# DMA transposes of the activations that read SBUF where they read a copy in HBM, with the last two blocks of channels overlapping

## The chip, the cores and the metric

The kernel runs on one core of a Trainium2 chip. The metric is device time in microseconds (us) from the first to the last instruction. Three runs of the kernel before gave 364.56, 364.61 and 364.64 us, a median of 364.61. The profiled execution, from which all durations below come, spans 364.9 us.

Engines: PE is TensorE (PEld its weight loads, which overlap with its matmuls), DVE is VectorE, ACT is ScalarE, POOL is GpSimd, SP is SyncE, which issues nearly all the DMAs of this kernel, one after the other in program order. SPq stands for SP's queue of instructions: the time that a DMA-issuing instruction holds SP.

## The reference

One sequence of 2048 tokens of 576 channels in bf16 goes through an attention block and an MLP block, each with a residual.

```python
def _A_ref(x, wqkv, wo):                 # x: layernormed input
    H = 32; Dh = D // H                  # D = 576, Dh = 18
    W, dil = 8, 2
    qkv = (x @ wqkv).reshape(B, S, 3, H, Dh).transpose(2, 0, 3, 1, 4)
    q, k, v = qkv[0], qkv[1], qkv[2]
    idx = pos[:, None] - off[None, :]    # off = 0, 2, ..., 14
    ...
    attn = softmax(where(mask, einsum("bhsd,bhswd->bhsw", q, kg) * Dh**-0.5, -1e9))
    return einsum("bhsw,bhswd->bhsd", attn, vg)... @ wo

def _B_ref(x, w1, b1, w2, b2):           # F = 4608
    h = gelu(layernorm(x) @ w1 + b1)
    return h @ w2 + b2

h  = x + _A_ref(layernorm(x), wqkv, wo)
h2 = h + _B_ref(layernorm(h), w1, b1, w2, b2)
```

## The kernel before

The 2048 tokens are 16 tiles of 128 tokens; token 16p + j is row p of tile j. A tile is handled with its tokens on the 128 partitions for layernorm, attention and the residual. Every matmul that contracts over the 576 channels (QKV, the output projection Wo, the first MLP product) needs the tile transposed: channels on the partitions, tokens in the free dimension. 576 is four blocks of 128 and one of 64. The kernel keeps a transposed tile as five blocks (`KT` = 5): four whole ones, and a fifth that holds channels 512 to 575 twice, once in each half of the partitions.

The matmuls work on halves of the PE array: each of them contracts 64 rows, and two of them, on the two halves of the rows (`half_rows(0)` and `half_rows(1)`), run beside each other into two different PSUM banks. `phase` (L210) issues them: in the first phase half r of the rows works for output half r, over five blocks; in the second the halves are swapped, over four blocks. The fifth block is needed in the first phase alone, and there each half of the partitions serves its own output half, which is why it holds the same 64 channels twice. The weights of these 64 channels lie in tiles of their own (`wqh_sb`, `woh_sb`, `w1h_sb`).

A transposed tile comes in one of two ways.

- On PE, for the eight even tiles of layernorm 1, the first two tiles of the attention output and the first two of layernorm 2: `transpose_in` (L178) makes five transposes of 128 columns into PSUM (L182), and where the source isn't yet doubled (`tail` is None) a sixth of 64 columns (L186). ACT or DVE copies the result to SBUF.
- By DMA, for the eight odd tiles of layernorm 1 (`xnT`), 14 tiles of the attention output (`oT`) and 14 of layernorm 2 (`hnT`). The tile is first stored to HBM with 640 columns: the 576 channels (L193, or L284 for two tiles of `xnT` at once) and then channels 512 to 575 again (L194, L285). A DMA transpose reads the 640 columns back into the five blocks (L199, L430, L493; L288 for two tiles). It waits for both stores.

Order of the work: `manual_schedule` leaves every engine's program order as written. The QKV stage (0 to 71 us) loops over pairs of (tile, q/k/v) products, numbered `qd` 0 to 23; tables list what is issued `after` each of them. `out_x(i)` and `in_x(i)` are the stores and the transpose of the i-th pair of odd tiles; the products of pair i begin at `qd` 12 + 3i. Loads of the MLP's weights are interleaved, each paced by an ACT instruction. From 71 us on, eight groups of two tiles pass through MLP1 (`pm`), Wo of the next group (`pw`) and MLP2 (`po`), with the attention of the group after that on DVE, its output tiles c and d sent by `send_o` and `read_o` and their layernorm 2 by `ln2_send` and `ln2_ins`. `oT` has three buffers, `hnT` one, `xnT` five of two tiles each.

Two orders in the code matter for the steps below. In groups 3 to 6 SP's program has `send_o(c)`, a load of the attention's window (`halo`), `read_o(c)`, `send_o(d)`, `read_o(d)`. In `ln2_in` (L492) the first transpose of a pair waits, by a dependency put in by hand, for the last store of the pair.

Of the kernel before, what the change touches and what calls it, by code (L numbers as in the profile page):

```python
# [17 lines left out]
def kernel(  # L18
# [71 lines left out]
    wq_sb = qp.tile([P, KF, 3 * D], BF16, name="wq_sb")  # L90
    wqh_sb = qp.tile([P, 3, HALF], BF16, name="wqh_sb")
# [24 lines left out]
    def load_wqkv_half(engine, t, r):  # L116
        c0 = t * D + r * HALF
        engine.dma_start(out=wqh_sb[half_rows(r), t, :], in_=A_wqkv[KF * P:D, c0:c0 + HALF])

    def load_wo(qs):  # L120
        src = A_wo.rearrange("(h d) c -> h d c", h=H)
        for q in qs:
            load(wo_sb[q * H:(q + 1) * H, :, :], src[:, q:4 * KF:4, :])
            load(woh_sb[q * H:(q + 1) * H, :], src[:, 4 * KF + q % 2, q // 2 * HALF:(q // 2 + 1) * HALF])

    def load_w1h():
        load(b1_bf[:], B_b1.rearrange("(ft p) -> ft p", p=P))
        src = B_w1[KF * P:D, :].rearrange("p (u g c) -> p u g c", u=NU, g=2)
        for r in range(2):
            load(w1h_sb[half_rows(r), :].rearrange("p (u c) -> p u c", u=NU), src[:, :, r, :])  # L130

    def load_w1(c):
        cols = slice(c * F // 6, (c + 1) * F // 6)
        load(w1_sb[:, :, cols], B_w1[0:KF * P, cols].rearrange("(k p) c -> p k c", p=P))
# [7 lines left out]
    def ln_stats(srcs, tag, c1, c0, bufs, first=None, eps=True):  # L142
        n = len(srcs)
        pool = qp if tag.startswith("ln1") else sb
        stats = pool.tile([P, n, 2, nc.vector.BN_STATS_DIM], F32, tag=f"{tag}_stats", name=f"{tag}_stats", bufs=bufs)
# [32 lines left out]
    def transpose_in(pt, src, tail=None):  # L178
        for kt in range(KT):
            c = min(kt * P, D - P)  # L180
            if kt < KF or tail is None:
                nc.tensor.transpose(pt[:, kt, :], src[:, c:c + P], ident[:])  # L182
        if tail is not None:
            nc.tensor.transpose(pt[:, KF, :], tail[:].rearrange("p r c -> p (r c)"), ident[:])
            return
        nc.tensor.transpose(pt[0:HP, KF, :], src[:, KF * P:D], ident[:])  # L186


    stored = [None]

    def dma_out(src):
        td = dram.tile([P, KT * P], BF16, tag="td", name="td", bufs=4)
        nc.sync.dma_start(out=td[:, 0:D], in_=src)  # L193
        stored[0] = nc.sync.dma_start(out=td[:, D:KT * P], in_=src[:, KF * P:D]).ins  # L194
        return td

    def dma_transpose(dst, src):
        td = dma_out(src)
        nc.sync.dma_start_transpose(out=dst, in_=td[:])  # L199
# [9 lines left out]

    def phase(duo, swap, after):  # L210
        first = last = None
        n = len(duo["g"][0])
        for i in range(n):
            for kt in range(KF if swap else KT):
                for r in range(2):
                    lhsT, rhs = duo["op"](r ^ swap, i, half_rows(r), kt)
# [36 lines left out]
    xnT, xn_tail = {}, {}  # L253
# [7 lines left out]
    def tr_x(js, tag):  # L261
        pair = psum_pair(tag or "CAB"[(ring_pos[0] + 1) % 3], "xt_pt", BF16)
        for n, j in enumerate(js):
            transpose_in(tr_view(pair, n), q_all[:, j, :], xn_tail.pop(j, None))
# [12 lines left out]
    xd = [dram.tile([2, P, KT * P], BF16, name=f"xd{i}") for i in range(NT // 4)]  # L277

    def odd_x(i):
        return q_all[:, 4 * i + 1:4 * i + 4:2, :]  # L280

    def out_x(i):
        dst = xd[i][:, :, :].rearrange("j p c -> p j c")
        nc.sync.dma_start(out=dst[:, :, 0:D], in_=odd_x(i))  # L284
        nc.sync.dma_start(out=dst[:, :, D:KT * P], in_=odd_x(i)[:, :, KF * P:D])  # L285

    def in_x(i):
        nc.sync.dma_start_transpose(out=new_xnT(ODD[2 * i:2 * i + 2])[:],  # L288
                                    in_=xd[i][:, :, :].rearrange("j p c -> (j p) c"))
# [10 lines left out]
    def qkv_duo(j, t):  # L300
        def make():
# [3 lines left out]
            def op(g, i, sl, kt):  # L305
                c0 = t * D + g * HALF
                return xt[sl, kt, :], (wq_sb[sl, kt, c0:c0 + HALF] if kt < KF else wqh_sb[sl, t, :])
# [118 lines left out]
    def send_o(j):  # L426
        o_sent[j] = dma_out(q_all[:, j, :])

    def read_o(j):
        nc.sync.dma_start_transpose(out=new_oT(j)[:], in_=o_sent.pop(j)[:])  # L430

    pw_of, o_sent = {}, {}

    def wo_duo(j, tag):
        def make():
# [3 lines left out]
            def op(g, i, sl, kt):  # L439
                c0 = g * HALF  # L440
                return t[sl, kt, :], (wo_sb[sl, kt, c0:c0 + HALF] if kt < KF else woh_sb[sl, :])
# [39 lines left out]
    def ln2_send(j):  # L481
# [3 lines left out]
        hn[j] = dma_out(y[:])  # L485

    def ln2_out(j):
        hn[j] = dma_out(hn[j][:])
# [3 lines left out]
    def ln2_in(j):  # L492
        read[0] = nc.sync.dma_start_transpose(out=hnT_slot(j), in_=hn.pop(j)[:]).ins  # L493
        if stored[0] is not None:
            tc.add_manual_dep(read[0], stored[0].name, sync_dep, reason="stores ahead of the transposes of LN2")
            stored[0] = None
# [45 lines left out]
    def mlp1_duo(grp, us, tag):  # L542
        def make():
# [5 lines left out]
            def op(g, i, sl, kt):  # L549
                f0 = fts[g][i] * P  # L550
                c0 = (GF * us[i // GF] + i % GF) * P
                return (w1_sb[sl, kt, f0:f0 + P] if kt < KF else w1h_sb[sl, c0:c0 + P]), ht[sl, kt, 0:N]
# [198 lines left out]
    with tc.manual_schedule(engines={ENG.PE, ENG.Activation, ENG.DVE, ENG.SP, ENG.Pool}):  # L751
        load_x(EVEN[0:1])
        load_x(EVEN[1:2])
        for r in range(2):
            load_wqkv_half(nc.scalar, 1, r)
# [6 lines left out]
        for r in range(2):  # L762
            load_wqkv_half(nc.sync, 2, r)
# [4 lines left out]
        for r in range(2):  # L768
            load_wqkv_half(nc.sync, 0, r)
# [25 lines left out]
        def center(j, mean, op):  # L795
            nc.vector.tensor_scalar(out=q_all[:, j, 0:D if j in EVEN[:5] else KF * P],
# [296 lines left out]
```

## Time and profile before

| engine | busy us | share of the span |
|---|---|---|
| PE | 357.1 | 98% |
| PEld | 291.4 | 80% |
| DVE | 302.3 | 83% |
| ACT | 229.2 | 63% |
| POOL | 37.1 | 10% |
| profiled execution, span | 364.9 | |
| median of three runs | 364.61 | |

| stretch, us | PE busy us | DVE busy us | DMA share | GB/s |
|---|---|---|---|---|
| 0 to 10 (start) | 8.21 | 5.46 | 0.79 | 234 |
| 10 to 38 (QKV, even tiles) | 27.47 of 28 | 25.66 | 0.93 | 263 |
| 38 to 71 (QKV, odd tiles) | 31.31 of 33 | 30.19 | 0.92 | 245 |
| 71 to 256 (groups 0 to 4) | 185.00 of 185 | 172.04 | 0.37 to 0.56 | 77 to 163 |
| 256 to 328 (groups 5 and 6) | 71.58 of 72 | 59.66 | 0.28 to 0.42 | 61 to 81 |
| 328 to the end | 33.57 of 37 | 9.32 | 0.05 | 15 |

The granted TensorE clock is 1.00 in every stretch. The first table is the busy time of each engine, a sum over its instructions; the second the same by stage. PE is nearly always busy: what can be won without removing PE work is what it idles, 364.9 - 357.1 = 7.8 us in all, and most of that lies at the start and the end.

### The profile page before, as it was taken

The page shows a single profiled execution, that of the slowest core. Times are in us where ns is not written, and L with a number is a line of the kernel's source. Part 1 is how long each engine was busy: PE and PEld are TensorE (multiplying, and loading weights), DVE is VectorE, ACT ScalarE, POOL GpSimd, SP SyncE. Part 2 cuts the span into 40 slices and gives each one's busy share as a digit, 9 for nine tenths or more (in the row PEclk, how much of TensorE's full clock was granted, in tenths as well). Part 3 has the DMA queues.
Part 4 walks back from the last instruction along what each step waited for, and adds up shares of the span by engine and source line. Part 5 has one row for each costly group of instructions (what it writes and reads, how often), then busy time and mean ns, then how long its engine had stood idle before and what let it go on. Part 6 is the DMA issues. An engine that isn't in the chain of part 4 may idle for free.

```text
span 364.9 us, 11410 instructions
## 1 busy us (share of the span) xinstructions
PE 357.1 (98%) x4891; PEld 291.4 (80%) x4891; DVE 302.3 (83%) x422; ACT 229.2 (63%) x507; POOL 37.1 (10%) x47
## 2 busy tenths in 40 slices
PE   8999799999999999999999999999999999999996
PEld 5678687788778878887888778877887788778874
DVE  5899989999899998999899989998799999710431
ACT  4779655799555684468646954695469366805630
POOL 2141003000111020101010211020101100100000
PEclk9999999999999999999999999999999999999999
DMA  7979998984436743531353155503642342120001
GB/s 226 300 153 330 239 238 184 359 286 73 136 103 88 178 178 77 82 110 51 85 121 88 37 131 91 87 35 92 131 64 59 74 84 72 37 56 19 2 2 33
DMA packets 61907, 43.70 MB, mean 120 GB/s; under 512 B 31888, under 2 KB 60176, under 8 KB 61856
## 3 DMA queue, kind: packets, MB, share of 16 engines
q1 hardware_dynamic: 59968, 41.13, 42.2%
q0 software_dynamic: 1728, 1.77, 4.6%
q8 instruction: 38, 0.62, 0.7%
q10 hardware_dynamic: 160, 0.07, 0.1%
q14 instruction: 13, 0.11, 0.1%
HBM read 21.10 MB, written 12.42 MB: 92 GB/s over the span
## 4 chain that ended last, share of the span: by engine, by line
PE 92%; DMA 5%; SPq 1%; ACT 1%; issue 0%; DVE 0%
PE pm L217 38%; PE po L664 26%; PE pq L217 12%; PE po L576 10%; PE pw L217 5%; DMA oT<-td 2%; DMA wq_sb<-in_A_wqkv_dram 1%; DMA xnT<-xd 1%; DMA xd<-q_all 1%; SPq L104 1%; PE xt_pt L182 1%; ACT kv_ring L312 0%; PE h_pt L182 0%; PE o_pt L182 0%; ACT q_all L175 0%
## 5 line engine op out<-in xcount | busy, mean ns | idle before, releaser
L557 ACT ACTIVATE h_all<-pm,b_sb 128x256 f16<-128x256 f32 (+1 forms) x288 | 108.5, 497 | 69.7 <-PE pm L217 69.7
L217 PE MATMUL pm<-hnT,w_sb 64*128 64x256 bf16 x2304 | 143.0, 269 | 0.0
L217 PEld LDWEIGHTS <-w_sb 64*128 64x128 bf16 x2304 | 111.8, 94 | 15.0 <-issue 1.7
L664 PEld LDWEIGHTS <-h_all 128*128 128x128 f16 x512 | 49.4, 98 | 14.0 <-issue 1.6
L217 PE MATMUL pq<-wq_sb,xnT 64*128 64x288 bf16 x768 | 54.7, 283 | 3.1 <-DMA xnT<-xd 2.2
L217 PEld LDWEIGHTS <-xnT 64*128 64x128 bf16 x864 | 43.1, 94 | 13.0 <-DMA xnT<-xd 2.5
L348 DVE TENSOR_TENSOR prod<-prod 128x2304 bf16<-128x2304 bf16 (+1 forms) x64 | 44.2, 691 | 2.0
L394 DVE TENSOR_TENSOR prod<-kv_ring,probs 128x4608 bf16<-128x4608 bf16 x16 | 40.9, 2555 | 2.4 <-DMA kv_ring<-kv_dram 2.0
L342 DVE TENSOR_TENSOR prod<-kv_ring,q_all 128x4608 bf16<-128x4608 bf16 x16 | 40.8, 2549 | 0.5 <-DMA kv_ring<-kv_dram 0.3
L217 PE MATMUL pm<-hnT,w1h_sb 64*128 64x256 bf16 x288 | 39.2, 269 | 0.0
L664 PE MATMUL po<-w2a_sb,h_all 128*128 128x288 bf16 (+1 forms) x282 | 38.9, 286 | 0.0
L400 DVE TENSOR_TENSOR prod<-prod 128x2304 bf16<-128x2304 bf16 (+1 forms) x32 | 33.9, 1058 | 1.1
L576 PEld LDWEIGHTS <-h_all 128*128 128x128 bf16 x288 | 27.9, 98 | 7.9 <-issue 1.0
L664 PEld LDWEIGHTS <-kv_ring 128*128 128x128 f16 x252 | 24.6, 98 | 6.3
L478 POOL TENSOR_TENSOR ln_rstd<-ln_var,mhalf 128x1 f32<-128x1 f32 x13 | 12.0, 924 | 171.1 <-ACT ln_var L477 171.1
L576 PE MATMUL po<-w2a_sb,h_all 128*128 128x288 bf16 x224 | 28.5, 286 | 0.0
L664 PE MATMUL po<-w2b_sb,h_all 128*128 128x288 bf16 (+1 forms) x142 | 21.3, 286 | 0.0
L217 PE MATMUL pw<-wo_sb,oT 64*128 64x288 bf16 x256 | 19.6, 283 | 0.4 <-DMA oT<-td 0.4
L735 ACT COPY po<-po 128x288 f32<-128x288 f32 x18 | 6.9, 384 | 19.7 <-PE po L664 18.6
L644 DVE TENSOR_TENSOR kv_ring<-h_all 128x1536 f16<-128x1536 f16 (+3 forms) x9 | 6.8, 752 | 14.7 <-ACT h_all L557 14.7
L162 POOL TENSOR_TENSOR ln_rstd<-ln_veps,mhalf 128x1 f32<-128x1 f32 (+2 forms) x14 | 13.4, 967 | 50.3 <-DVE ln_veps L156 34.7
L217 PEld LDWEIGHTS <-oT 64*128 64x128 bf16 x288 | 13.6, 94 | 5.0 <-DMA oT<-td 1.2
(110 smaller groups left out, 387.3 us busy)
## 6 DMA issues: line engine op xcount, KB each, us to landing
w_sb<-in_B_w_dram SPq DMA_DIRECT2D x6, 768.0 KB, 5.9
kv_ring<-kv_dram SPq DMA_DIRECT2D x28, 144.0 KB, 2.8
w2a_sb<-in_B_w_dram SPq DMA_DIRECT2D x4, 1008.0 KB, 6.2
kv_dram<-kv_ring SPq DMA_DIRECT2D x13, 288.0 KB, 3.3
out_dram<-o_sb SPq DMA_DIRECT2D x15, 144.0 KB, 2.6
td<-q_all SPq DMA_DIRECT2D x14, 144.0 KB, 1.8
td<-hn SPq DMA_DIRECT2D x14, 144.0 KB, 1.8
x_all<-in_A_x_dram SPq DMA_DIRECT2D x12, 144.0 KB, 2.9
```

Source lines behind the costliest of these rows:

```text
L162: nc.gpsimd.tensor_tensor(out=rstd[:], in0=veps[:], in1=mhalf[:].to_broadcast([P, n]), op=ALU.pow)
L217: last = nc.tensor.matmul(duo["g"][r ^ swap][i], lhsT=lhsT, rhs=rhs, start=(swap == 0 and i == 0 and kt == 0), stop=(swap == 1 and kt == K ...
L342: nc.vector.tensor_tensor(out=prod[:], in0=k_ring[j % 2], in1=q_all[:, j, :].unsqueeze(1) .to_broadcast([P, W, D]), op=ALU.mult)
L348: nc.vector.tensor_tensor(out=prod[:, :, o * H:o * H + n], in0=prod[:, :, a * H:a * H + n], in1=prod[:, :, c * H:c * H + n], op=ALU.add)
L394: nc.vector.tensor_tensor(out=prod[:].rearrange("p w (d h) -> p w d h", h=H), in0=v_ring[j % 2].rearrange("p w (d h) -> p w d h", h=H), in ...
L400: nc.vector.tensor_tensor(out=prod[:, 0:n, :], in0=prod[:, 0:n, :], in1=prod[:, n:2 * n, :], op=ALU.add)
L478: nc.gpsimd.tensor_tensor(out=rstd[:], in0=var[:], in1=mhalf[:], op=ALU.pow)
L557: pace[0] = nc.scalar.activation(out=hT(grp)[:, f, 0:N], in_=ps[:, r, i * N:(i + 1) * N], func=ACT.Gelu_apprx_tanh, bias=b1_sb[:, f:f + 1] ...
L576: nc.tensor.matmul(banks[half], lhsT=hT(grp)[:, f, i * P:(i + 1) * P], rhs=w2_rows(f)[:, half * HALF:(half + 1) * HALF], start=(f == 0), s ...
L644: nc.vector.tensor_tensor(out=s_slot(t, m0, m1), in0=a, in1=b, op=alu)
L664: nc.tensor.matmul(bank, lhsT=l, rhs=r, start=start, stop=stop, skip_group_check=True)
L735: nc.scalar.copy(out=bank[seed[step][1]], in_=bank[seed[step][0]])
```

## The change

The DMA transposes read their tile in SBUF, without stores to HBM. Since the source has 576 columns and a transposed block has 128, each tile takes two instructions: columns 0 to 511 into blocks 0 to 3, and columns 448 to 575 into block 4. Channels 448 to 511 now are the ones held twice, in the upper half of block 3 and in the lower half of block 4. `transpose_in` makes five whole transposes for every tile on PE, and the sixth, of 64 columns, is gone.

`block(r, kt)` says which block half r of the rows reads at step kt, so that every product still has nine matmuls per half. The weights follow: `wq_sb` has a fifth block with rows 448 to 575 (one load of 128 partitions for two of 64 partitions and half the columns); `wo_sb` and `w1_sb` hold channels 512 to 575 in the upper half of their block 3, and `woh_sb` and `w1h_sb` hold channels 448 to 511. The load of `w1` is cut in four pieces of 864 KB with three blocks each and two pieces of 576 KB on 64 partitions, for six of 768 KB; the load of `wo` has two more DMAs.

On SP, a transpose is issued where the store was, or where the transpose was, as the diff shows. In SP's program the transposes of pair 0 of the odd tiles stand ahead of four stores of k and v to HBM, where the stores `out_x(0)` were. The dependency by hand in `ln2_in` is gone. The DVE writes each centred even tile in one instruction, where three of them had a second one for the doubled tail, and the statistics of layernorm 1 share buffers.

```diff
-    wq_sb = qp.tile([P, KF, 3 * D], BF16, name="wq_sb")
-    wqh_sb = qp.tile([P, 3, HALF], BF16, name="wqh_sb")
+    wq_sb = qp.tile([P, KT, 3 * D], BF16, name="wq_sb")
...
-    def load_wqkv_half(engine, t, r):
-        c0 = t * D + r * HALF
-        engine.dma_start(out=wqh_sb[half_rows(r), t, :], in_=A_wqkv[KF * P:D, c0:c0 + HALF])
+    def load_wqkv_last(engine, t):
+        engine.dma_start(out=wq_sb[:, KF, t * D:(t + 1) * D], in_=A_wqkv[D - P:D, t * D:(t + 1) * D])
...
     def load_w1(c):
-        cols = slice(c * F // 6, (c + 1) * F // 6)
-        load(w1_sb[:, :, cols], B_w1[0:KF * P, cols].rearrange("(k p) c -> p k c", p=P))
+        if c < 4:
+            cols = slice(c * F // 4, (c + 1) * F // 4)
+            load(w1_sb[:, 0:KF - 1, cols], B_w1[0:(KF - 1) * P, cols].rearrange("(k p) c -> p k c", p=P))
+        else:
+            r = c - 4
+            load(w1_sb[half_rows(r), KF - 1, :], B_w1[(KF - 1) * P + r * P:(KF - 1) * P + r * P + HP, :])
...
-    def transpose_in(pt, src, tail=None):
+    def transpose_in(pt, src):
         for kt in range(KT):
             c = min(kt * P, D - P)
-            if kt < KF or tail is None:
-                nc.tensor.transpose(pt[:, kt, :], src[:, c:c + P], ident[:])
-        if tail is not None:
-            nc.tensor.transpose(pt[:, KF, :], tail[:].rearrange("p r c -> p (r c)"), ident[:])
-            return
-        nc.tensor.transpose(pt[0:HP, KF, :], src[:, KF * P:D], ident[:])
+            nc.tensor.transpose(pt[:, kt, :], src[:, c:c + P], ident[:])
...
-    def dma_out(src):
-        td = dram.tile([P, KT * P], BF16, tag="td", name="td", bufs=4)
-        nc.sync.dma_start(out=td[:, 0:D], in_=src)
-        stored[0] = nc.sync.dma_start(out=td[:, D:KT * P], in_=src[:, KF * P:D]).ins
-        return td
-
     def dma_transpose(dst, src):
-        td = dma_out(src)
-        nc.sync.dma_start_transpose(out=dst, in_=td[:])
+        nc.sync.dma_start_transpose(out=dst[:, 0:KF, :], in_=src[:, 0:KF * P])
+        return nc.sync.dma_start_transpose(out=dst[:, KF:KT, :], in_=src[:, D - P:D]).ins
...
+    def block(r, kt):
+        return kt if kt < KF - 1 else KF - 1 + (r ^ (kt == KF))
...
-    def out_x(i):
-        dst = xd[i][:, :, :].rearrange("j p c -> p j c")
-        nc.sync.dma_start(out=dst[:, :, 0:D], in_=odd_x(i))
-        nc.sync.dma_start(out=dst[:, :, D:KT * P], in_=odd_x(i)[:, :, KF * P:D])
-
     def in_x(i):
-        nc.sync.dma_start_transpose(out=new_xnT(ODD[2 * i:2 * i + 2])[:],
-                                    in_=xd[i][:, :, :].rearrange("j p c -> (j p) c"))
+        js = ODD[2 * i:2 * i + 2]
+        new_xnT(js)
+        for j in js:
+            dma_transpose(xnT[j], q_all[:, j, :])
...
     def ln2_in(j):
-        read[0] = nc.sync.dma_start_transpose(out=hnT_slot(j), in_=hn.pop(j)[:]).ins
-        if stored[0] is not None:
-            tc.add_manual_dep(read[0], stored[0].name, sync_dep, reason="stores ahead of the transposes of LN2")
-            stored[0] = None
+        read[0] = dma_transpose(hnT_slot(j), hn.pop(j)[:])
...
-        for r in range(2):
-            load_wqkv_half(nc.scalar, 1, r)
+        load_wqkv_last(nc.scalar, 1)
...
-            6: [c_(ln1_rstd, 10), c_(ln1_act, 8, 1), c_(halo, A[0], 1), c_(out_x, 0)],
+            6: [c_(ln1_rstd, 10), c_(ln1_act, 8, 1), c_(halo, A[0], 1), c_(in_x, 0)],
...
-            8: [c_(att_qk_a, A[1]), c_(att_qk_rest, A[1], 1), c_(ln1_act, 8, 3), c_(in_x, 0), c_(out_x, 1)],
+            8: [c_(att_qk_a, A[1]), c_(att_qk_rest, A[1], 1), c_(ln1_act, 8, 3)],
...
-                m1[0] += [c_(pv_sum, c), c_(send_o, c), c_(pv_sum, d), c_(read_o, c), c_(send_o, d), c_(read_o, d)]
+                m1[0] += [c_(pv_sum, c), c_(dma_tr_o, c), c_(pv_sum, d), c_(dma_tr_o, d)]
```

## The prediction

> **What bounds the kernel now.** I read first the page's busy times, then who waited for whom on PE, then the chain of waits, and last the timeline of SP with the groups of the transposes.
>
> ```profile
> PE 357.1 (98%) x4891; PEld 291.4 (80%) x4891; DVE 302.3 (83%) x422; ACT 229.2 (63%) x507; POOL 37.1 (10%) x47
> ```
>
> PE is the bound: 7.8 us of the 364.9 are idle. The waits of PE say which of these are a DMA's:
>
> ```profile
> PE pq L217 <- DMA xnT<-xd: 2.2, 1, 2.2
> PE pq L217 <- DMA wq_sb<-in_A_wqkv_dram: 0.9, 3, 0.4
> PE pw L217 <- DMA oT<-td: 0.4, 2, 0.2
> ```
>
> (us in total, times, longest.) Transposes that come by DMA cost PE 2.2 + 0.4 = 2.6 us and no more: `hnT` isn't in the list at all. The chain (start us, us, what) shows where, and the other places that the change touches:
>
> ```profile
> 4.22 5.41 DMA wq_sb<-in_A_wqkv_dram
> ...
> 9.68 0.68 PE pq L217 x6
> 10.36 0.39 PE xt_pt L182 x5
> 10.74 0.17 PE xt_pt L186
> ...
> 29.57 0.77 ACT q_all L175
> 30.34 0.07 SPq L284
> 30.41 0.05 issue
> 30.46 3.78 DMA xd<-q_all
> ...
> 34.32 5.33 DMA xnT<-xd
> 39.64 0.05 issue
> 39.69 1.40 PE pq L217 x20
> ...
> 308.14 2.74 DMA oT<-td
> 310.88 0.05 issue
> 310.93 1.77 PE pw L217 x26
> ```
>
> The reader is to see three things: PE starts its steady work at 9.68, when a weight load lands; the sixth transpose of a tile on PE (L186) is 0.17 us of the chain; and at 39.69 PE has waited for a store and a transpose, 9.3 us from 30.34, one after the other. What one such transfer costs SP and when it lands:
>
> ```profile
> 306.10 0.34 SPq L193 DMA_DIRECT2D td<-q_all  x1
> 306.49 0.42 SPq L194 DMA_DIRECT2D td<-q_all  x1
> 308.14 1.21 SPq L430 DMA_TRANSPOSE oT<-td  x1
> ```
>
> ```profile
> L493 SPq DMA_TRANSPOSE hnT<-td x14: 1206/1222/1275, 103.6 to 321.4; - x14
> L288 SPq DMA_TRANSPOSE xnT<-xd x4: 1331/1416/1525, 34.3 to 54.3; - x4
> ```
>
> (SP held, ns, least/median/most.) A transpose holds SP 1.21 us for 128 rows and 1.42 for 256, and lands 2.74 us after its start in the chain's last case, so 1.5 after SP is free. The stores before it cost 2.0 us more.
>
> **The change part by part.**
>
> *Sixth transpose on PE.* Nine are removed. Two (at 5.2 and 5.8) lie ahead of the wait that ends at 9.68 and are worth nothing; seven are in the chain: 7 x 0.17 = -1.2 us. The three tail writes removed from DVE are worth nothing: PE runs without a wait through 12 to 28 us, and covers them.
>
> *First pair of odd tiles.* Its transposes now start when ACT has finished the second tile, 30.4. There are four, and no row shows a transpose with its source in SBUF. From below, it costs what a store from SBUF costs (0.34 us of SP); from above I see no bound but twice the row of HBM, 2.4. I take 1.2 as the mean hold h of an instruction, the row it is nearest to: same operation, same queue, fewer columns. The first tile is then there at 30.4 + 2.4 + 1.5 = 34.3, perhaps 2.5 later behind the weight load that is in flight (the row's 5.33 against 2.74), and PE wants it at 37.5: -2.2 us.
>
> *Second pair.* SP is held longer ahead of it: 4 x 1.2 to 35.2, the four stores of k and v now behind the transposes (2.7 us, as in the row at 31.02 of SP's timeline), a window load and a load of `w1` (0.45 and 1.33), so its transposes start at 39.7 where they started at 40.57. PE needs it at 46.34 - 2.2 + 0.2 = 44.3 (the 0.2 is the start's delay below, less three of the 0.17). Alone the first tile would land at 39.7 + 2.4 + 1.5 = 43.6; but the transposes of this pair took 3.8 us before, behind a `w1` load that is now issued 0.9 us later and is 864 for 768 KB (0.4 us at that stage's 245 GB/s). That puts both tiles at 44.4 + 1.3 = 45.7, and the first about 0.9 ahead, at 44.8. I take a new wait of 0.5 us, with 0 and 1.5 as its ends. Pairs 2 and 3 are wanted some 8 and 16 us after pair 1 and stay covered.
>
> *Start.* The 36 KB halves of `wqh_sb` become 144 KB blocks: 72 KB more on ACT's queue ahead of the load that ends at 9.63 (72 KB at 263 GB/s, 0.3 us), and the block of v right after it, 144 KB or 0.6 us, which PE needs from the second pair of steps on, at 9.80. So 9.63 + 0.3 + 0.6 = 10.5, +0.7 us; ends 0.3 (block four comes in the shadow) and 1.0. Nothing covers it: PE is in the chain from there.
>
> *`oT`.* In groups 5 and 6 the second tile misses PE by 0.2 us. Group 6 is the tightest: source ready at 306.10, PE wants it at 310.7, so two instructions plus 1.5 us fit for h up to 1.55. At 1.2 it lands at 310.0, and both waits go: -0.4 us (up to -1.0 if PEld's 0.5 us each counts).
>
> *`hnT`.* Four instructions for four stores and two transposes: SP 4.8 us against 5.6 in all, but the first transpose no longer waits for the pair's last store. The cover is PE's MLP2. Tightest is group 0: SP is free for them at 100.8, the pair wanted at 109.28: h up to 1.7. Worked the same way (source ready or SP free, plus 4h, plus 1.5, against the start of `pm`), groups 2, 3 and 4 stand h up to about 1.8, 2.0 and 2.0. Zero.
>
> *Loads.* `wo` has two more DMAs (0.85 us of SP near 22, used at 52 us). The last `w1` piece is issued near 58 and needed at 71; the largest load of the page (1152 KB) landed in 10.2. Zero, with 3 us of cover. What is queued behind the longer transposes on SP (window loads, outputs) is wanted by DVE much later than PE's tiles.
>
> *Sum.* 364.9 - 1.2 - 2.2 + 0.5 + 0.7 - 0.4 = 362.3 for the execution profiled, which stood 0.3 above the median of the runs: **362.0 us**. The ends of the terms give 364.6 - 1.2 - 2.2 + 0.3 - 1.0 = 360.5 and 364.6 - 1.2 - 2.2 + 1.5 + 1.0 - 0.2 = 363.5.
>
> [...] The rows say 1.5 to 1.9 us to landing for most stores of the main loop and 2.7 to 4.9 for the transposes. [...]
>
> **The rivals.**
>
> *The transposes hold SP longer than from HBM (slower).* One mechanism, at SP: a tile needs two instructions, and four in a row stand ahead of each pair. The waits appear in this order: second pair of odd tiles (from h = 1.3, and six times as steep as h), `oT` of group 6 (1.55), `hnT` of group 0 (1.7). At h = 2.0: pair 1 starts at 30.4 + 8 + 2.7 + 1.8 = 42.9 and its first tile lands at 48.4 against 44.3, +4.1, its second +1.2; `oT` +0.9; `hnT` +1.0 and +0.8. That is +8.0 on 364.6 - 1.2 - 2.2 - 0.4 + 0.7 = 361.5: **369.5**. It turns where 3.1 us of waits are made, near h = 1.75. For it speaks that 256 rows cost only 0.2 us more than 128, so the hold is mostly per instruction and cutting one in two doubles it; against it that 1.75 is almost half more than the median row of 128 rows.
>
> *The wait moves one pair on.* The second pair's tiles land behind `w1` and the stores as late as the first pair's did: 2.2 us come back, 361.5 + 2.2 = **363.7**. For it: the DMA share of 0.92 to 0.93 in this stage. Against: the transposes no longer wait for their own stores.
>
> *The `w1` pieces on 64 partitions land after 71 us*, or the start costs more than 1 us: about **366**. Against: the 13 us of cover above.
>
> **How the numbers follow.** Forecast 0.55; wait moved on 0.12; SP held longer 0.27; late weights and the rest 0.06. Under about 0.2% a measurement can't tell a change of this kernel from none, so same is 363.9 to 365.3: a third of the second case's spread and the part of the third near its turning point, 0.08. Faster is the forecast and the rest of the second case, 0.62; slower 0.30. The likeliest case's own range is 360.5 to 363.5; that and the second hold 0.67, and to leave out no more than 2 in 10 the range goes up to 368, h near 1.9.
>
> **What would show it.** Right: PE's waits list no `xnT` at the first pair and under 1.5 us at the second, no `oT`; a wait for `wq_sb` at the start longer by 0.3 to 1 us; no L186; a transpose holds SP 1.6 us or less in the mean. Wrong: a hold over 1.75, waits of PE for `hnT` or for several `oT`, or idle PE at 71 us for `w_sb`.

## The result, and the profile after

The changed kernel took 366.96 us (median of 4 executions, 365.55 to 367.43), the kernel before beside it 364.59 (363.62 to 364.64): a ratio of 1.0068, 95% interval 1.0044 to 1.0092. It is slower by 2.4 us, where 2.6 us less were forecast. A second series gave 367.23 (8 executions) and 1.0081 (1.0053 to 1.0109). The ratios in this document are of fast executions alone; the medians and ranges hold all executions, so a ratio need not be the quotient of two medians.

The page's busy times of the changed kernel, in the execution that was profiled first (span 363.8, time 365.55):

```profile
PE 357.1 (98%) x4882; PEld 292.1 (80%) x4882; DVE 301.5 (83%) x419; ACT 229.0 (63%) x507; POOL 35.7 (10%) x47
```

Nine instructions of PE are gone, as the diff says, yet PE is as busy as before. Who waited for whom on PE, in the same execution (total, times, longest):

```profile
PE pq L213 <- DMA xnT<-q_all: 1.5, 1, 1.5
PE xt_pt L187 <- DVE q_all L769: 0.6, 1, 0.6
PE pm L213 <- DVE o_sb L719: 0.3, 1, 0.3
```

No `oT` and no `hnT` is in the list. There is one wait for `xnT`, and the chain of waits (start, us, what) tells which pair of odd tiles it is:

```profile
6.77 4.62 PE pq L213 x42
...
19.25 21.09 PE pq L213 x343
40.34 5.76 DMA xnT<-q_all
...
46.15 3.60 PE pq L213 x56
```

It is the second pair, whose first transpose starts on SP at 40.34. The first line explains the busy time: 42 products took 4.62 us at the start, where the last line has 56 of them in 3.60. The second trace, below, doesn't have this. The slow start also hides part of the wait: PE comes to the second pair at 44.6 us here, and at 43.5 in the second trace.

The time of a run is its span and 1.7 to 1.9 us more, in every run that lists both (365.55 and 363.8; 367.17 and 365.4). By this the execution of the kernel before that the prediction was worked from, span 364.9, would have taken 366.7 us (an estimate; its own time isn't on record): it was one of the rare long ones, not one 0.3 from the median. Of 149 other executions of this kernel 13 took over 366. A second trace of the unchanged kernel (`ctl_before`, span 362.3, time 364.06) has these waits of PE for DMAs, and no others:

```profile
PE pq L217 <- DMA wq_sb<-in_A_wqkv_dram: 0.5, 2, 0.3
PE pw L217 <- DMA oT<-td: 0.2, 1, 0.2
```

The 2.2 us of `xnT` that the change was to remove are not there. They are most of the 2.6 us by which the two spans differ: 2.2 for `xnT`, 0.4 for `wq_sb` and 0.2 for `oT`, less 0.2 of PE's work. A second trace of the changed kernel (`rep_after`, span 365.4) can be set against it term by term:

```profile
PE pq L213 <- DMA xnT<-q_all: 3.4, 1, 3.4
PE pq L213 <- ACT q_all L300: 0.8, 1, 0.8
...
PE xt_pt L187 <- DVE q_all L769: 0.5, 1, 0.5
PE pq L213 <- DMA wq_sb<-in_A_wqkv_dram: 0.5, 2, 0.2
PE pm L213 <- DVE o_sb L719: 0.3, 1, 0.3
PE pq L213 <- ACT xnT L268: 0.2, 1, 0.2
```

PE's busy time fell from 357.3 to 355.5 (-1.8), its idle time rose from 362.3 - 357.3 = 5.0 to 365.4 - 355.5 = 9.9 (+4.9). The list holds this: `xnT` 3.4, ACT's `q_all` 0.8 (there ACT writes q over the tiles that the transposes read; that it waited for them is likely, but not shown), the start 0.7 (0.5 + 0.2 for DVE and ACT), `o_sb` 0.3, less 0.2 of `oT`. Of the 1.8 us of work 0.55 lie in the first 10 us (8.00 busy against 8.55), where they make up for nearly all of the longer waits. So the gain of the change was had, and a new wait cost more.

### The profile page after: what moved, and what is told of

The parts are those of the page before. It is cut to its first block, busy times and chain, and to the rows that moved or that the text cites. A ratio compares the mean times of both kernels' runs of the same rounds, so it can differ in the third digit from the quotient of the medians.

```text
span 363.8 us, 11362 instructions
## 1 busy us (share of the span) xinstructions
PE 357.1 (98%) x4882; PEld 292.1 (80%) x4882; DVE 301.5 (83%) x419; ACT 229.0 (63%) x507; POOL 35.7 (10%) x47
## 4 chain that ended last, share of the span: by engine, by line
PE 82%; DVE 12%; DMA 4%; issue 0%; POOL 0%; ACT 0%; DVEq 0%; POOLq 0%
PE pm L213 33%; PE po L640 26%; PE pq L213 13%; PE po L552 5%; PE pw L213 4%; DVE prod L336 3%; DVE prod L382 2%; DVE prod L330 2%; DMA xnT<-q_all 2%; DMA kv_ring<-kv_dram 1%; DVE prod L388 1%; PE xt_pt L187 1%; DMA x_all<-in_A_x_dram 1%; DVE peak L349 1%; DVE logits L343 0%; DVE logits L350 0%
## 5 line engine op out<-in xcount | busy, mean ns | idle before, releaser
L213 PEld LDWEIGHTS <-w_sb 64*128 64x128 bf16 x2304 | 113.2, 94 | 14.2 <-issue 2.2
L213 PE MATMUL pq<-wq_sb,xnT 64*128 64x288 bf16 x864 | 57.4, 288 | 1.5 <-DMA xnT<-q_all 1.5
L213 PEld LDWEIGHTS <-xnT 64*128 64x128 bf16 x864 | 42.1, 96 | 14.0 <-DMA xnT<-q_all 1.8
L552 PE MATMUL po<-w2a_sb,h_all 128*128 128x288 bf16 x224 | 28.5, 286 | 0.0
L168 POOL TENSOR_TENSOR ln_rstd<-ln_veps,mhalf 128x1 f32<-128x1 f32 (+2 forms) x14 | 12.4, 895 | 51.2 <-DVE ln_veps L162 28.8
```

The costliest lines, as they stand in the source:

```text
L168: nc.gpsimd.tensor_tensor(out=rstd[:], in0=veps[:], in1=mhalf[:].to_broadcast([P, n]), op=ALU.pow)
L213: last = nc.tensor.matmul(duo["g"][r ^ swap][i], lhsT=lhsT, rhs=rhs, start=(swap == 0 and i == 0 and kt == 0), stop=(swap == 1 and kt == K ...
L552: nc.tensor.matmul(banks[half], lhsT=hT(grp)[:, f, i * P:(i + 1) * P], rhs=w2_rows(f)[:, half * HALF:(half + 1) * HALF], start=(f == 0), s ...
```

## The experiments

The kernel before, timed beside each group of these, had medians of 364.2 to 364.5.

| kernel | median us (range, executions) | ratio to before, 95% interval | span traced |
|---|---|---|---|
| `ctl_before` | 364.48 (363.80 to 368.43, 12) | 1.0016 (0.9988 to 1.0044) | 362.3 |
| `rep_after` | 367.23 (366.37 to 369.04, 8) | 1.0081 (1.0053 to 1.0109) | 365.4 |
| `e1_copy_new_layout` | 366.64 (364.62 to 369.18, 12) | 1.0053 (1.0024 to 1.0082) | 362.8 |
| `e2_order` | 364.64 (363.42 to 368.08, 12) | 0.9995 (0.9964 to 1.0026) | 362.1 |
| `e3_w1_behind` | 368.71 (367.91 to 369.42, 10) | 1.0093 (1.0062 to 1.0123) | 367.1 |
| `e4_both` | 365.80 (365.10 to 366.90, 12) | 1.0015 (0.9985 to 1.0046) | 364.9 |
| `e5_copy_six` | 366.94 (364.17 to 369.94, 12) | 1.0050 (1.0015 to 1.0085) | 367.0 |
| `e6_w1_later` | 364.96 (363.10 to 367.05, 12) | 1.0020 (0.9999 to 1.0041) | 361.3 |
| `e7_three` | 366.25 (364.47 to 368.43, 12) | 1.0050 (1.0030 to 1.0071) | 364.2 |
| `e9_halo` | 364.67 (363.49 to 366.88, 12) | 1.0015 (0.9993 to 1.0037) | 362.6 |
| `e10_halo_order` | 364.58 (363.43 to 368.15, 12) | 1.0005 (0.9977 to 1.0032) | 366.4 |
| `e11_split` | 365.36 (363.17 to 371.18, 12) | 1.0002 (0.9971 to 1.0033) | 362.9 |
| `e12_odd_by_copy` | 363.08 (362.41 to 368.30, 12) | 0.9971 (0.9945 to 0.9998) | 361.4 |
| `e13_odd_direct` | 366.49 (365.37 to 368.33, 10) | 1.0057 (1.0037 to 1.0078) | 364.8 |

### Both kernels again

`ctl_before` and `rep_after` are the two kernels as they are.

> The kernel before, again, to see spans and clocks of every run. Theory A (the change is slower by what lies outside the span): its device time is no more than 0.5 us above its span, where the changed kernel's is 1.75 above. Theory B (the changed kernel is slower because the granted clock falls below 1.0 in most of its runs): its clock is 1.000 in all runs, and its spans all 364 to 365. Theory C (the two kernels differ by less than a chip's or a session's scatter): spans and clocks scatter as the changed kernel's do, 363.8 to 365.6.

> The changed kernel, again. Theory A: device time 1.7 to 1.8 us above the span in every run. Theory B: clock 0.995 and a span of 365 to 365.6 in most runs, 1.000 and 363.8 in the few others; ratio to before 1.003 to 1.009. Theory C: ratio with an interval that holds 1.

The difference holds. It doesn't lie outside the span: the time is 1.7 to 1.9 us above the span in every execution of both. Nor does it need a lower clock: the four executions of `rep_after` with a mean granted clock of 1.00 took 366.37 to 367.17 us. The traces are those compared above: the base of the prediction's sum was an untypical execution.

### The layout without the direct transposes

`e1_copy_new_layout` keeps the new layout of blocks, weights and loads, and takes every transposed tile through HBM in SP's order of before (`dma_out` stores 512 columns and then the last 128):

```diff
 def dma_transpose(dst, src):
-    nc.sync.dma_start_transpose(out=dst[:, 0:KF, :], in_=src[:, 0:KF * P])
-    return nc.sync.dma_start_transpose(out=dst[:, KF:KT, :], in_=src[:, D - P:D]).ins
+    td = dma_out(src)
+    nc.sync.dma_start_transpose(out=dst, in_=td[:])
...
```

> The changed kernel's layout of weights and blocks, its loads and its five transposes on PE, with the copy in HBM and the order of SP as before (the copy has channels 0 to 511 and 448 to 575). If the route of the transposes makes the difference: time as before, 364.6, less the 1.2 us of the sixth transposes and plus some tenths for the start, 363.5 to 364.2, clock 1.000. If the loads and the layout make it: as the changed kernel, 366.5 to 367.

`e5_copy_six` is the same with `w1` in six column pieces, as before, each of three DMAs.

```diff
-        if c < 4:
-            cols = slice(c * F // 4, (c + 1) * F // 4)
+        cols = slice(c * F // 6, (c + 1) * F // 6)
...
```

> The kernel with the copy in HBM and the new layout (366.6), with w1 loaded in six pieces of columns as before, each by three DMAs (768 KB in all, as before), for four pieces of 864 KB and two of 576 KB on 64 partitions. Theory L: time falls to 363.5 to 364.5, that of before less the sixth transposes. If the cut of w1 doesn't matter: 366 to 367 as it was.

Both are 2.3 to 2.5 us above the kernel before, so the new cut of `w1` is not the cause. By its expectation e1 speaks for the loads and the layout as a whole. But `e2_order`, `e9_halo` and `e12_odd_by_copy`, below, have the same loads and layout and are level with the kernel before or faster, so these alone don't make the loss. The trace of e1 (its fastest execution) shows what the missing PE work turned into: PE waits 0.8 for `xnT` and 1.0 for `oT`, where `ctl_before` had 0 and 0.2. PE arrives earlier and the copies don't. This makes up for the trace's span. The trace of e5 is one of its long executions (span 367.0). PE waits 1.6 us for `oT` in it, and 2.8 at the first pair of odd tiles:

```profile
39.60 2.37 PE L219 MATMUL pq<-wq_sb,xnT 64*128 64x288 bf16 x20 [2.76 <-DMA xnT<-xd]
```

So in some executions the copies through HBM are waited for there too. Why the median of e1 lies 2 us above its traced execution is not settled.

### SP's order

`e2_order` moves the four transposes of the first pair behind the four stores of k and v, two steps later:

```diff
-            6: [..., c_(halo, A[0], 1), c_(in_x, 0)],
+            6: [..., c_(halo, A[0], 1)],
-            8: [..., c_(ln1_act, 8, 3)],
+            8: [..., c_(ln1_act, 8, 3), c_(in_x, 0)],
```

> The changed kernel with one move in SP's program: the four transposes of the first pair of odd tiles stand behind the four stores of k and v (where the transpose of before stood), not ahead of them. Theory Q (the queue: the window load behind them waits for these stores, and the second pair's transposes for it): the second pair starts 1 to 2 us earlier, PE's wait for xnT falls from 1.5 to 3.4 us to under 1, time 364.5 to 366. Theory H (four instructions of 1.22 us hold SP too long whatever the order): the wait only moves to the first pair, time 366.5 to 367.5. Theory L (the loads of the weights, larger and on 64 partitions): no change, 367.2.

It regains 2.6 us of `rep_after`'s median. SP's timeline from the four stores on (start, time that SP is held, what), first in the kernel before (`ctl_before`):

```profile
30.04 2.59 SPq L298 DMA_DIRECT2D kv_dram<-kv_ring  x4
33.64 1.40 SPq L288 DMA_TRANSPOSE xnT<-xd  x1
...
36.26 0.48 SPq L339 DMA_DIRECT2D kv_ring<-kv_dram  x1
...
39.78 1.33 SPq L288 DMA_TRANSPOSE xnT<-xd  x1
```

In the changed kernel (first trace):

```profile
34.63 2.05 SPq L286 DMA_DIRECT2D kv_dram<-kv_ring  x4
38.58 0.32 SPq L327 DMA_DIRECT2D kv_ring<-kv_dram  x1
38.99 1.26 SPq L103 DMA_DIRECT2D w_sb<-in_B_w_dram  x1
40.34 1.21 SPq L191 DMA_TRANSPOSE xnT<-q_all  x1
```

The same places in `e2_order`:

```profile
29.46 2.51 SPq L286 DMA_DIRECT2D kv_dram<-kv_ring  x4
32.02 1.34 SPq L191 DMA_TRANSPOSE xnT<-q_all  x1
...
37.32 0.68 SPq L327 DMA_DIRECT2D kv_ring<-kv_dram  x1
38.10 0.39 SPq L103 DMA_DIRECT2D w_sb<-in_B_w_dram  x1
38.54 1.22 SPq L191 DMA_TRANSPOSE xnT<-q_all  x1
```

The window load (L327) reads what the stores write, so it waits until they have landed, and SP waits with it. In the kernel before, SP came to it 3.6 us after the stores, and they had landed: it started at 36.26, 0.1 us behind the instruction ahead of it. In the changed kernel the stores leave SP at 36.68 and the load starts at 38.58: 1.9 us in which SP issues nothing (2.2 and 3.1 in `rep_after` and `after_look`), while the second pair's transposes stand in the queue. SP's list of waits in `rep_after`, 28 to 66 us, names the cause (the wait of 4.1 is an earlier window load's):

```profile
SPq L327 <- DMA kv_dram<-kv_ring: 6.3, 2, 4.1
```

In `e2_order` the transposes of the first pair, 5.2 us from 32.02 on, fill the time in which the stores land, and the load starts 0.1 us behind them.

`e9_halo` tries that wait alone: the changed kernel, with this one window load behind the second pair's transposes.

```diff
-             9: [c_(halo, A[1], 1), c_(ln1_act, 9, 0)],
+             9: [c_(ln1_act, 9, 0)],
-            10: [..., c_(in_x, 1)],
+            10: [..., c_(in_x, 1), c_(halo, A[1], 1)],
```

> The changed kernel with one window load moved: the one issued between the k/v stores and pair 1's transposes, which waits on SP until those stores have landed (issued 40.70 where the stores ended on SP at 38.45), goes behind pair 1's transposes. Theory 'that wait on SP is what the prediction's working missed': pair 1's transposes start 1.5 to 2.5 us earlier than in the changed kernel's profiles (40.34 and 41.60) and PE's wait for xnT is under 1 us; the window load lands about 5 us later, so DVE may be late at 57 us (a wait for DVE at o_pt like the 2.8 us of e3_w1_behind), time 364.5 to 367.5. Rival 'the four transposes' own 4.9 us on SP are enough': pair 1 starts within 1 us of before and PE waits for xnT 1.5 us or more, time 366.5 to 369.5.

The second pair starts at 39.26, 1.1 to 2.3 earlier than in the changed kernel's traces, DVE isn't late, and the median is 364.67: 2.3 to 2.6 below the changed kernel. The trace's wait for `xnT` is 1.7, not under 1 as expected, nearer to the rival in that; but it ends at 45.03 where the changed kernel's ends at 46.15, 46.44 and 46.84. So one load that stood on SP until the stores had landed was worth most of the loss, but not all that PE waits for.

### The w1 load ahead of the second pair

`e3_w1_behind` (the changed kernel) and `e4_both` (`e2_order`) put the third load of `w1` one step later, behind the second pair's transposes; `e6_w1_later` (`e2_order`) three steps later (12 in place of the 10 below), behind a window load too.

```diff
-        loads = {v: ... for c, v in enumerate((3, 4, 9, 13, 15, 17))}
+        loads = {v: ... for c, v in enumerate((3, 4, 10, 13, 15, 17))}
```

> The changed kernel with the third load of w1 issued behind the second pair's transposes, not ahead of them. If these transposes land late because that load's 864 KB are ahead of them: PE's wait for xnT falls by 1 us or more, time 365 to 366.3. If they are late because SP comes to them late: the wait falls by the 0.4 to 1.3 us that this load holds SP, time 366 to 367.

> Both moves in one. Theory Q: PE waits for no xnT at the second pair, and the time is that of before less the sixth transposes (1.2 us) plus a later start (0.3 to 0.7): 363.5 to 364.5. Theory H: 366 or more.

In both the wait for `xnT` at the second pair shrinks or goes (0.9 us at three places in e3, none in e4), and another of 2.8 us takes its place. So e3 comes out above both of its expectations, e4 between its two. PE's timeline of `e4_both`, with the wait ahead of the instruction in brackets:

```profile
56.70 0.44 PE L187 MATMUL o_pt<-ident,q_all 128*128 128x128 bf16 x5 [2.76 <-DVE h L440]
```

The window load issued behind 864 KB of `w1` lands 6.7 us after its issue in e4, where that of `e2_order` took 2.4; DVE waits 3.6 us for it, and PE for DVE.

> First pair's transposes behind the four k/v stores as in e2_order, and besides the third load of w1 (864 KB) issued behind the window load that follows pair 1, ahead of pair 2's transposes, instead of ahead of pair 1's. In e2_order PE waits 1.1 us for xnT at pair 1 with that load ahead of it; in e4_both it waits none for xnT but 2.8 us for DVE, whose window load was queued behind the w1 load. Theory 'SP's queue order and what is in flight ahead of the transposes is all that the direct transposes cost': neither wait here, PE idle for xnT under 0.3 us and for L187 under 0.8, span 361.0 to 361.6, time about 363, ratio 0.994 to 0.998 (the prediction's 1.2 us of sixth transposes is then seen). Rival 'the removed PE work is given back wherever it is removed': a wait of about 1 us turns up elsewhere (pair 2's xnT, or DVE), time 364.3 to 365, ratio 0.999 to 1.002.

The traced execution is as the first theory had it: no wait for `xnT`, span 361.3. The median is not: 364.96, with executions from 363.10 to 367.05. Three more traces of the same program and one of the changed kernel were to tell what differs:

> The same program as e6_w1_later, another execution. Theory 'the landing of the direct transposes varies with the w1 and w2 loads that are in flight': where the span is over 362.5, PE's list of waits has xnT, hnT or oT with the missing time (span less 361.3 within 0.5 us). Rival 'DVE's window loads vary': waits for DVE tiles (h, o_sb, kv_ring, h_all) hold it. Rival 'the clock': PE's busy time is over 355.7 by the difference.

> As e6b_look: the same program once more, with the same three readings of the difference to 361.3.

> As e6b_look: the same program once more, with the same three readings of the difference to 361.3.

> The changed kernel as it is, a third execution with a trace. Expected: pair 1's first transpose starts at 40 to 42, PE waits 1.5 to 4 us for xnT at 46 to 47 us and little else over 0.8 us; span 364 to 366. If the wait is under 1 us and the span still over 364, the queue on SP isn't what separates the medians.

| trace | PE waits for `xnT`, us | PE busy, us | span |
|---|---|---|---|
| `e6_w1_later` | 0 | 355.7 | 361.3 |
| `e6c_look` | 0.5 | 356.2 | 362.2 |
| `e6d_look` | 1.5 | 357.4 | 363.9 |
| `e6b_look` | 2.6 | 356.5 | 364.8 |

The span grows with the wait for `xnT`, but the wait doesn't hold the whole difference within 0.5 us, as the first theory wanted: PE's busy time has another 0.5 to 1.7. In `e6d_look` these are slow products at the start (46 in 4.68 us), as in the first trace of the changed kernel. Where the wait falls, in `e6b_look` on PE's timeline:

```profile
39.01 1.03 PE L213 MATMUL pq<-wq_sb,xnT 64*128 64x288 bf16 x13 [1.11 <-DMA xnT<-q_all]
63.38 1.40 PE L213 MATMUL pq<-wq_sb,xnT 64*128 64x288 bf16 x20 [1.52 <-DMA xnT<-q_all]
```

At the first pair and at the last, not at the second, which the move was for; in `e6c_look` and `e6d_look` it falls at the last. `after_look` (span 365.7) waits 2.6 at the second pair, as expected. What all have in common is SP: from 28 to 61 us its instructions hold it for 16.3 us in `ctl_before`, 5.8 of them transposes, and for 27.5 to 29.0 us in the three traces of the changed kernel, 21.9 to 22.4 of them transposes.

`e10_halo_order` is `e2_order` with the window load of `e9_halo` moved as well; `e11_split` in addition issues the third `w1` load in halves, the second three steps later.

> e2_order and e9_halo together: pair 0's transposes behind the four k/v stores, and the window load that stood between pair 0's and pair 1's transposes behind pair 1's. SP ahead of pair 1 then has the stores (2.6), four transposes (5.1) and one w1 load (0.5): pair 1 should start at 37.7 to 38 (38.54 in e2_order, 39.26 in e9_halo), 0.7 earlier than in e2_order, where PE waited 1.1 for xnT. Theory 'the wait is the sum of what stands ahead on SP': wait for xnT at pair 1 0 to 0.5, median 363.6 to 364.4, ratio 0.997 to 1.000. Rival 'the landing behind 864 KB of w1 decides, not the start': the wait stays at 1 us or more, ratio 1.000 to 1.003.

> e10_halo_order with the third load of w1 cut in two halves of 432 KB, the first where it was (ahead of pair 1's transposes), the second behind the window loads, ahead of pair 2's. Theory 'what w1 bytes are in flight ahead of the transposes sets their landing': 432 KB less at 390 GB/s is 1.1 us earlier at pair 1, so no wait there; median 0.3 to 1.0 below e10_halo_order, ratio 0.995 to 0.999. Rival 'bytes moved to a later pair are waited for there' (as in the looks at e6, at pair 3): a wait for xnT of 0.5 to 1.5 us at pair 2 or 3, ratio 1.000 to 1.004.

Neither gains on `e2_order` (ratios 1.0005 and 1.0002). The 390 GB/s of the second expectation are a rate of short stretches: slices of 0.2 us have 375 to 430 in `ctl_before` from 27.0 to 29.6 us, and the 8 us from 27 to 35 have 330 in the mean. In the trace of e11 PE waits 0.3 at the second pair and 0.8 at the fourth; the one of e10, its slowest execution, has 1.3 at the second, which starts at 39.66 and not at 37.7 to 38, and 2.5 at the fourth. The rivals are nearer. In these traces what is taken from one pair is waited for at another.

### The cover in the main loop

`e7_three` is `e2_order` with three transposes instead of two for each tile of `oT` and `hnT`.

```diff
-    def dma_transpose(dst, src):
-        nc.sync.dma_start_transpose(out=dst[:, 0:KF, :], in_=src[:, 0:KF * P])
+    def dma_transpose(dst, src, cuts=(0, KF)):
+        for k0, k1 in zip(cuts, cuts[1:]):
+            nc.sync.dma_start_transpose(out=dst[:, k0:k1, :], in_=src[:, k0 * P:k1 * P])
...
-        dma_transpose(new_oT(j)[:], q_all[:, j, :])
+        dma_transpose(new_oT(j)[:], q_all[:, j, :], (0, 2, KF))
...
-        read[0] = dma_transpose(hnT_slot(j), hn.pop(j)[:])
+        read[0] = dma_transpose(hnT_slot(j), hn.pop(j)[:], (0, 2, KF))
```

> e2_order with the wide transpose of each oT and hnT tile cut in two (three instructions per tile of 1.21 us of SP each, 3.65 us per tile, as if the mean hold of two were 1.82); xnT as in e2_order. Theory 'the cover in the main loop is as the prediction computed it' (oT of group 6 late from 1.55, hnT of group 0 from 1.7): PE waits for oT 0.5 us longer than in e2_order (0.2), hnT 0.5, together about +1 us: time 365 to 366.5, ratio 1.001 to 1.006. Rival 'the main loop has cover beyond that, the 1.82 hold costs nothing': waits as in e2_order, ratio 0.997 to 1.002. Rival 'other queues on SP suffer (window loads, outputs)': more than 2 us, ratio over 1.006, with waits of PE for DVE.

The median rose by 1.6 us, as the first theory said, but not by its way: the trace has `oT` at 0.3 (0.2 in `e2_order`), no `hnT`, and 0.8 us of waits for DVE's tiles in MLP2 that e2 hasn't. So the cover for `hnT` is larger than computed, and the longer hold is paid for elsewhere. What makes DVE late is not shown.

### One half of the change at a time

`e12_odd_by_copy` is the changed kernel with the odd tiles through HBM, in the order of before, and `oT` and `hnT` straight from SBUF. `e13_odd_direct` is the reverse, in the order of `e2_order`.

```diff
 # e12
 def in_x(i):
-    js = ODD[2 * i:2 * i + 2]
-    new_xnT(js)
-    for j in js:
-        dma_transpose(xnT[j], q_all[:, j, :])
+    nc.sync.dma_start_transpose(out=new_xnT(ODD[2 * i:2 * i + 2])[:],
+                                in_=xd[i][:, :, :].rearrange("j p c -> (j p) c"))
...
```

> The changed kernel with the four pairs of odd tiles by way of HBM, as before (one transpose of 256 rows per pair, SP held about 6 us for them instead of 21), oT and hnT straight from SBUF. Theory 'the cost lies with the odd tiles alone': against e1_copy_new_layout (366.64, PE waits 1.0 for oT) the waits for oT go, xnT stays at 0.3 to 0.8, median 364.5 to 366, and 1 to 2.5 below the changed kernel's 367. Rival 'the direct transposes cost in the main loop too': waits for hnT, oT or DVE there, median 366.5 or more.

> The other cell: odd tiles straight from SBUF in the order of e2_order, oT and hnT by way of HBM as before. Theory 'the cost lies with the odd tiles alone, and oT direct gains its 0.2 to 1.0': waits for oT of 0.2 to 1.0 come back, xnT as in e2_order (0 to 1.5), median 364.6 to 365.6, that is 0 to 1 above e2_order. Rival 'the direct transposes cost in the main loop': median below e2_order's 364.64 by 0.5 or more.

| median us | `oT`, `hnT` through HBM | `oT`, `hnT` direct |
|---|---|---|
| odd tiles through HBM | 366.64 (`e1_copy_new_layout`) | 363.08 (`e12_odd_by_copy`) |
| odd tiles direct, order of `e2_order` | 366.49 (`e13_odd_direct`) | 364.64 (`e2_order`) |
| odd tiles direct, order of the change | | 366.96, 367.23 |

Direct `oT` and `hnT` gain in both rows, 3.6 and 1.9 us; in both the intervals of the two ratios don't overlap. Direct odd tiles gain nothing in the left column (0.15). In the right one they lose 3.9 to 4.2 us in the order of the change, clear of noise too. The 1.6 us that they lose in the order of `e2_order` are not: the intervals of 0.9971 and 0.9995 overlap. The only wait of PE for transposed tiles in `e12_odd_by_copy`:

```profile
PE pq L213 <- DMA xnT<-xd: 0.9, 2, 0.6
```

The waits for `oT` that the copies make are gone, and `xnT` costs less than in any trace of the changed kernel. In `e13_odd_direct` both are there, 1.9 for `xnT` and 1.3 for `oT`. The traces of e1 and e12 differ by 1.4 us, 1.0 of it `oT`; why their medians differ by 3.6 is not shown. e12 is the only version whose interval lies below 1: 0.9971 of the time before, 0.9945 to 0.9998, a small gain and barely clear.

## Why the prediction was wrong

*The base of the sum: the step that failed first.* The sum was made on a span of 364.9 "which stood 0.3 above the median of the runs". That set a span beside times. The execution was some 2.1 us above the median (the estimate above), and the wait of 2.2 us at the first odd pair, largest term of the sum, was most of what made it so. `ctl_before`, whose time of 364.06 is a common one, doesn't have that wait and can't lose it. (The changed kernel doesn't wait at the first pair in any of its traces, as forecast.) Made on its span, without that term and with 0.2 us of `oT`, the same steps give 362.3 - 1.2 + 0.5 + 0.7 - 0.2 = 362.1, a time of 363.9: some 0.15% below the runs, no change that could be told.

*"I take a new wait of 0.5 us" at the second pair: mis-sized, and this made the kernel slower.* It is 1.5, 3.4 and 2.6 us in three traces. The queue in the text was the right one (transposes, stores, window load, `w1`, transposes), but the window load was priced at its 0.45 us of SP. That SP stands with it until the stores have landed, 1.9 to 3.1 us, was left out. Smaller errors went the other way: the first pair's transposes start at 28.5 to 29.3, 0.1 us behind the window load ahead of them, and not at 30.4, and `w1` holds SP for 0.4 us in two of the traces, not 1.33. Together the second pair starts at 40.3 to 41.6 and not at 39.7; from there to the end of the wait it takes 5.2 to 5.8 us, where 5.1 was taken. And PE is there at 43.5 in `rep_after`, 0.8 earlier than the 44.3 of the prediction, because the start costs nothing (below). `e2_order` and `e9_halo`, which take the wait on SP out in two ways, come back to the level of before.

*The terms as measured.* From `ctl_before` to `rep_after`: -1.2 (sixth transposes) + 3.4 (second pair) + 0.8 (ACT's `q_all`) + 0.3 (`o_sb`) - 0.2 (`oT`) = +3.1 us, the difference of their spans. The 0.8 and the 0.3 are not in the prediction; the other two traces of the changed kernel have the 0.3 alone.

*"Pairs 2 and 3 ... stay covered": right for the changed kernel, by little.* Its three traces have one wait for `xnT` each, at the second pair, and it delays PE for the pairs behind. With the second pair earlier, PE waits 0.5 to 2.5 us at the last one in five traces (three of e6, e10, e11), and not in `e2_order` and `e9_halo`. SP is held for about 28 of the 33 us in which all four pairs pass.

*The hold: right.* 1.2 us was taken. The groups of the transposes in the changed kernel (SP held, ns: least, median, most):

```profile
L191 SPq DMA_TRANSPOSE oT<-q_all x14: 1208/1212/1795, 81.5 to 305.3; - x14
L192 SPq DMA_TRANSPOSE oT<-q_all x14: 1222/1224/1432, 82.8 to 306.6; - x14
```

512 columns hold SP as long as 128: 1.212 and 1.224 us in the median. The 16 transposes of `xnT` hold it longer, 1.37 us in the mean (21.95 in all), with single ones of 2.1 and 2.4. So the rival of a longer hold falls. What decides in these traces is the number of instructions: four for a pair that took one, and 4.9 us of SP (the second pair in the first trace) for 1.4 (the median of before).

*Sixth transposes: right.* -1.2 was forecast on the path; PE's busy time fell by 1.8 in the trace at full speed, 0.55 of it at the start. In the traces of e1 and e13 that gain is waited away again.

*Start: wrong.* +0.7 was forecast, for weights that land later. PE's waits for `wq_sb` are 0.5 us in both `ctl_before` and `rep_after`. All waits ahead of the steady work did grow by 0.7, from 0.5 to 1.2 us, but for DVE's first tile and ACT's copy, and PE had 0.55 us less work there. It comes to its next transposes at the same time, in `ctl_before` and then in `rep_after`:

```profile
10.20 0.45 PE L182 MATMUL xt_pt<-ident,q_all 128*128 128x128 bf16 x5
```

```profile
10.18 0.45 PE L187 MATMUL xt_pt<-ident,q_all 128*128 128x128 bf16 x5
```

So the term is nothing on the path; that the waits sum to the forecast 0.7 is luck.

*`oT` and `hnT`: right.* None of the three traces has a wait for either. That `oT` would be worth more than 0.4 (the table of halves) wasn't foreseen: the waits that the copies make in e1, e5 and e13, 1.0 to 1.6 us, are not in the trace of before.

*The rival "the wait moves one pair on"* named where the wait went, not why: it is SP's wait for the stores. Its price, 363.7, had the same wrong base and the wait at its old size. None of the prediction's signs of being wrong (a longer hold, `hnT`, several `oT`, `w_sb` at 71 us) came: the loss lay where it didn't look.

## What to carry to other kernels

Before a wait in a profile is counted as a gain, see whether the typical execution has it: set the profiled run's own time, not its span, beside the median. When DMAs are added to a queue that issues in order, price for what stands behind them not only their hold but every later instruction of the queue that waits for a landing (here one window load, 1.9 to 3.1 us). A change that helps at one place of a queue and hurts at another is worth splitting: here one half of it was better than all, and slightly better than none.

## What the runs showed of the hardware

After some waits PE ran slowly for a while. `after_look` and `rep_after`, PE's timeline where the second pair is waited for:

```profile
46.44 5.28 PE L213 MATMUL pq<-wq_sb,xnT 64*128 64x288 bf16 x56 [2.56 <-DMA xnT<-q_all]
```

```profile
46.84 3.60 PE L213 MATMUL pq<-wq_sb,xnT 64*128 64x288 bf16 x56 [3.36 <-DMA xnT<-q_all]
```

The same 56 products took 1.68 us more after the shorter wait. The stretches of `after_look` around it (us, busy time of PE, PEld, DVE, ACT and POOL with the numbers of their instructions, granted clock, DMA share, GB/s) say why:

```profile
44.00:46.40 2.40, 0.00 (x0) 0.00 (x0) 2.23 (x4) 0.62 (x2) 0.00 (x0) 1.00 1.16 284
46.40:50.00 3.60, 3.56 (x36) 2.53 (x38) 1.64 (x4) 0.63 (x1) 0.00 (x0) 0.61 0.51 86
```

The granted clock was 0.61 in the 3.6 us behind the wait; in `rep_after` it stayed at 1.00. The other long waits of PE in the kept traces, with the granted clock in the 3.6 us behind each:

| trace | PE waits, us | granted clock behind it |
|---|---|---|
| `e5_copy_six` | 2.76 (`xnT`) | 0.54 |
| `e4_both` | 2.76 (DVE) | 0.63 |
| `e3_w1_behind` | 2.75 (DVE) | 0.53 |
| `e10_halo_order` | 2.49 (`xnT`) | 0.62 |
| `before` | 2.22 (`xnT`) | 1.00 |
| `e13_odd_direct` | 1.90 (`xnT`) | 1.00 |

Five of the six waits of 2.49 us and more were followed by a low clock, and none of the shorter ones. So a wait of this length cost two thirds of itself again in `after_look` (1.68 us after 2.56), and nothing in `rep_after`, whose 3.36 us are the longest of these waits. What decides between the two is not shown. The slow products at 6.77 in the changed kernel's first trace (42 in 4.62 us, where `e5_copy_six` took 3.28 for as many) are alike in effect, though the granted clock is shown as 1.00 there.
